# Reciprocal square roots of an attention and MLP kernel, computed as powers on GpSimd in place of a guess and refining steps on VectorE

## The chip, the cores and the metric

The kernel runs on one core of one Trainium2 chip. The metric is the device time of one execution in microseconds (us); the lower, the better. A core has five engines that run side by side, each working through its own instructions in order: TensorE (PE in the profile: matrix products, with the weight loads as PEld), VectorE (DVE), ScalarE (ACT), GpSimd (POOL) and SyncE (SP, which here only starts transfers). They wait for each other by semaphores. Transfers between the chip's main memory (HBM) and the on-chip memory (SBUF), and the transposes in SBUF, run on 16 DMA engines.

## The reference

Attention over 8 batches, 12 heads, 448 tokens and 64 values a head, with q and k normalised, and behind it a gated MLP. What matters here are the two places with a reciprocal square root:

```python
def rmsnorm(x, g):
    rms = np.sqrt(np.mean(x * x, axis=-1, keepdims=True) + 1e-06)
    return x / rms * g
q_n, k_n = (rmsnorm(q, g_q), rmsnorm(k, g_k))
scores = scale * np.matmul(q_n, k_n.transpose(0, 1, 3, 2))
...
mu = np.mean(v, axis=-1, keepdims=True)
var = np.mean((v - mu) ** 2, axis=-1, keepdims=True)
v_n = (v - mu) / np.sqrt(var + 1e-06) * g_ln
```

The first is taken over 64 values for every token and head of q and k, the second over the 512 values of the MLP's v half for every token. Everything is float32.

## The kernel before

The work goes over 48 pairs of heads, six to a batch. A pair has 896 rows of q and 896 of k, as 14 columns of 128 partitions by 64 values. For a pair:

- `squares` (L324, L325): ACT squares the 896 values of each partition, DVE adds them to 14 sums, the tile `ss`.
- `norms` (L335 to L337): the sums of two pairs at a time, 28 columns, become reciprocal roots `ny`. Only the first two pairs are done singly, with 14 columns, so it runs 25 times. On DVE: a scale and add (L335), a guess from the bits of the number in two integer instructions (L107, L108), and seven refining instructions (`newton`, L112 to L118). The tiles are `nx` (the mean square), `ni` (its bits), `nt` (between) and `ny`.
- `split` (L344 to L352): POOL multiplies k by the product of the two gains (L344) and q and k by the roots (L345). ACT takes the float16 high part (L347), POOL the rest (L348), and DVE copies parts into place (L350, L351). A DMA transpose on SP's queue makes `qt` of `hl` (L352). For the first pair all of POOL's part is done on DVE.
- `scores` (L411 to L436): PE multiplies (L411), DVE takes the maximum of a row (L414), ACT the exponential and its sum (L416), DVE the reciprocal of the sums (L420, L422). The high part of the weights is made by ACT (L432) or, for three or four of seven tiles, by POOL (L430), the rest by DVE (L433), and a transpose on SP's queue makes `at` (L436).
- `pv` (L453, L455): PE multiplies the weights with v; ACT and DVE split the result into `xh` and `xl` (L461, L462).

The MLP of a batch (`moe`) runs beside the attention of the next one, a few steps per pair; for the last batch it follows directly. Its `layernorm` takes means and variances (L532, L533, L541 to L545) and then the reciprocal root of four columns, with the same ten DVE instructions: L553, L107, L108, L112 to L118, in the tiles `lx`, `li`, `lt`, `ly`. It runs eight times. L560 applies mean and root, L562 and L563 split the result, and L605 multiplies it. L575 is the product for the other half, u, beside which the layernorm runs.

A third user of the guess, `pow2_scale` (L107, L108, L133 to L135), takes a power of two from it and has no refining steps.

No order of the instructions is written out. The program is traced in the order in which the loops at its end interleave the streams (scores, pv, weights, MLP), each instruction with a place in that order. A planner then simulates the engines with its own costs and puts each engine's instructions into the queue by place and by when they become ready. So a change in one place can move instructions in others.

Of the kernel before, what the change touches and what calls it, by code (L numbers as in the profile page):

```python
# [8 lines left out]
F32 = mybir.dt.float32  # L9
# [13 lines left out]

# places in the order of the work that the MLP and its gelus are moved by
MOFF, MOFF0, GP = 200, 100, 350
# steps of the weights and of the MLP per pair of heads (first, second, middle, last batch)
WR, M0, M1, MR, ML = 3, 8, 7, 11, 11
# pairs of heads at which the first MLP begins and by which the weights are done
I0, WD = 5, 6
# tiles of the scores that share a reciprocal; that are transposed together; whose high part GpSimd  # L30
# makes (in the first batch)
RG = ((0, 2), (2, 4), (4, 7))
TG = (2, 2, 2, 1)
PT, PT0 = (0, 3, 6), (0, 2, 4, 6)
# buffers
NS, NV, NM = 4, 1, 3
# [8 lines left out]
def kernel(  # L45
# [45 lines left out]

# [1 line left out]
    ones = const.tile([P, P], F32, name="ones")  # L93
    G.memset(ones, 1.0)
    ident = const.tile([P, P], BF16, name="ident")
    make_identity(nc, ident)
# [13 lines left out]
    def newton(y, x, t):  # L110
        """y, a guess of x ** -0.5 within 3.5%, made better by a step of third and one of second order."""
        V.tensor_tensor(out=t, in0=x, in1=y, op=ALU.mult)  # L112
        V.tensor_tensor(out=t, in0=t, in1=y, op=ALU.mult)
        V.scalar_tensor_tensor(out=t, in0=t, scalar=-10.0 / 3.0, in1=t, op0=ALU.add, op1=ALU.mult)
        V.scalar_tensor_tensor(out=y, in0=t, scalar=5.0, in1=y, op0=ALU.add, op1=ALU.mult)
        V.scalar_tensor_tensor(out=t, in0=x, scalar=-0.5 * 0.375 ** 3, in1=y, op0=ALU.mult, op1=ALU.mult)
        V.tensor_tensor(out=t, in0=t, in1=y, op=ALU.mult)
        V.scalar_tensor_tensor(out=y, in0=t, scalar=1.5 * 0.375, in1=y, op0=ALU.add, op1=ALU.mult)  # L118

    def pow2_scale(name, part, pool):  # L120
        """part [rows, n] holds sums of squares. Gives the power of two that takes
        every element of the tensor below 2^14 * 1.04, and its inverse."""
        rows, n = part.shape
# [13 lines left out]

# [1 line left out]
    W = {}  # L139

    def decode(dst, raw, tmp):
        """float64 words (low, high) to float32; magnitudes below float32's normal range give 0."""
        hi, lo = raw[:, :, 1], raw[:, :, 0]
# [9 lines left out]
    def weights():  # L153
        nonlocal mlp
        ctx_w = ExitStack()
        # w_in's parts take the place of its float32 values, one K block after the other
        wi = const.tile([P, KT, 2, DF], F16, name="wi")
# [44 lines left out]

        # w_sg with its rows and columns in the order of the tokens on chip, and the
        # last 64 columns twice, so that both halves of the partitions get them
        wsr = [mlp.tile([P, S], F32, name="wsr", tag="ug", bufs=5) for c in range(CK)]
# [48 lines left out]

# [1 line left out]
    # A head's tokens on chip: 128 c + p is token 3 p + c for c < 3 (blocks m0, m1, m2), 384 + p the  # L256
    # tail t. A pair of heads A, B is 7 columns of 128 rows: A's m0, m1, m2, then the tails of A and B
    # in one, then B's m0, m1, m2; so A's keys are in the order (m0, m1, m2, t), B's in (t, m0, m1, m2).
    R = {}
# [31 lines left out]
    def load_v(i):  # L291
        """A head's v in 7 columns: m0, m1, m2, (t, m0a), (m0b, m1a), (m1b, m2a), (m2b, t), with a and b
        the halves of a block: what meets the blocks of A's transposed weights and, from (t, m0a) on, of B's."""
        if i >= NI:
# [16 lines left out]
    def v8(x):  # L311
        """Of a pair's columns A's 0..3 and B's 3..6."""
        return bass.AP(tensor=x.tensor, offset=x.offset, ap=[list(x.ap[0]), [10 * D, 2], [1, 4 * D]])
# [13 lines left out]
    def norms(i, cnt):  # L327
        gi, j = divmod(i, NG)
        n = cnt * SSW
        ss = SS[gi].rearrange("p a b -> p (a b)")[:, j * SSW:j * SSW + n]  # L330
        x, t = (sml.tile([P, NG * SSW], F32, name=f"n{c}", bufs=2)[:, 0:n] for c in "xt")
        si = sml.tile([P, NG * SSW], I32, name="ni", bufs=2)[:, 0:n]
        yt = sml.tile([P, NG * SSW], F32, name="ny", bufs=3)
        y = yf = yt[:, 0:n]
        V.tensor_scalar(out=x, in0=ss, scalar1=1.0 / D, scalar2=1e-6, op0=ALU.mult, op1=ALU.add)  # L335
        rsqrt_guess(yf, si, x)
        newton(yf, x, t)  # L337
        for j in range(cnt):
            R[i + j]["rs"] = y[:, j * SSW:(j + 1) * SSW]
# [17 lines left out]
    def vsquares(i):  # L357
        """The sums of squares of the GV pairs of heads from i on."""
        if i >= NI:
# [29 lines left out]
    def parts_of(t):  # L389
        """Tile t of a pair's 896 rows of scores: (rows of the tile, head)."""  # L390
        if t == CM:
# [73 lines left out]

# [1 line left out]
    def cluster(acts, done):  # L467
        """Gelu activations, one behind the other from when the last one's operand is ready."""
        p = tc.cur_priority
# [15 lines left out]
    def moe(b, early=False):  # L485
# [5 lines left out]
        mv = sml.tile([P, CK, 2], F32, name="mv", bufs=2)  # L491
        # the last 64 tokens have the first half of v in the lower partitions, the second in the upper
        tiles = [(slice(t * P, (t + 1) * P), slice(t * DH, (t + 1) * DH)) for t in range(CM)]
        tiles.append((slice(SM, S), slice(CM * DH, CM * DH + FH)))
        # K block by K block while the batch's last heads are still to come, tile by tile otherwise
        steps = [(t, g) for t in (CM, *range(CM)) for g in range(NP)]
# [39 lines left out]
        def layernorm():  # L536
# [12 lines left out]
            x = sml.tile([P, CK], F32, name="lx", bufs=2)  # L549
            si = sml.tile([P, CK], I32, name="li", bufs=2)  # L550
            y = sml.tile([P, CK], F32, name="ly", bufs=2)
            tt = sml.tile([P, CK], F32, name="lt", bufs=2)
            V.tensor_scalar(out=x, in0=mv[:, :, 1], scalar1=1e-6, scalar2=None, op0=ALU.add)  # L553
            rsqrt_guess(y, si, x)
            newton(y, x, tt)
            vh = mlp.tile([P, CM * DH + FH], F16, name="vh")
# [64 lines left out]
        if b % 2 == 0:  # L621
# [4 lines left out]
            GT[b] = gth, gtl, xt  # L626
        # the last 64 tokens of two batches go together
        for t in range(CM + b % 2):
# [37 lines left out]

# [1 line left out]
    def low(gen, off):  # L668
        """The instructions of a generator, `off` places later in the order."""
        def run():  # L670
# [125 lines left out]
```

## Time and profile before

| what | value |
|---|---|
| median of three runs | 1049.12 us |
| lowest and highest run | 1044.31 and 1051.55 us |
| span of the profiled execution, first to last instruction | 1047.2 us |
| mean granted TensorE clock in it | 0.903 |
| instructions in it | 17092 |
| moved by DMA | 177.74 MB, mean 170 GB/s |
| HBM read and written | 54.58 and 11.01 MB |

The profiled execution's own time is known by its span; what lies around the span is not shown apart from it. The three runs lie 0.7% apart.

How to read the lines that follow: a group's line has the line of the kernel, the engine, the operation, the tile written and the tiles read, the shapes and the count, and then the busy time in us, the mean of one instruction in ns, and the engine's idle time just ahead of such instructions with what ended it. The view by line or tile gives three durations in ns, least, median and greatest, and the first and last start. The view by stage gives the busy time of each engine in a stretch, with the number of instructions in brackets. A timeline row gives start and duration in us, engine, line, operation and tiles. A row of waits gives who waited for whom, the sum in us, how often, and the longest.

### The profile page before, as it was taken

The numbers are of one execution on the slowest core, as the hardware profiler recorded it, in microseconds if no ns is written. First come the engines' busy times: TensorE is split into PE (matmuls) and PEld (weight loads), VectorE is DVE, ScalarE is ACT, GpSimd is POOL, SyncE is SP. The second block draws the span as 40 slices with busy tenths as digits, with TensorE's granted clock in tenths as the row PEclk, the third lists the DMA queues.
The fourth block names the chain that finished last, engine by engine and source line by source line (L and its number), as shares of the span: only waits on it lengthen the run. The fifth ranks groups of instructions, "written<-read, shape, count | busy, mean of one in ns | idle before, by whom it ended". The sixth has DMA issues, their size and how long they took to land. (4 is left out here: it accounts for less than half of the span.)

```text
span 1047.2 us, 17092 instructions
## 1 busy us (share of the span) xinstructions
PE 809.6 (77%) x5652; PEld 447.3 (43%) x5652; DVE 899.9 (86%) x1959; ACT 705.4 (67%) x1418; POOL 504.6 (48%) x435
## 2 busy tenths in 40 slices
PE   0333556757689798888979899887979799799998
PEld 0111222424454346444644357343634365346546
DVE  4999979999789997999979998999889988999430
ACT  2565787676677777677767767587667686877441
POOL 1777745637536463443545372545455443535021
PEclk9666688888899899899999899999989999999999
DMA  5969589685989979996797879994989779838501
GB/s 144 254 174 244 125 179 215 160 185 108 207 180 206 194 156 206 173 217 152 162 213 181 167 149 196 202 211 106 207 190 195 148 166 201 180 89 174 110 1 61
DMA packets 528217, 177.74 MB, mean 170 GB/s; under 512 B 472257, under 2 KB 521985, under 8 KB 528129
## 3 DMA queue, kind: packets, MB, share of 16 engines
q1 hardware_dynamic: 484928, 144.07, 66.6%
q10 hardware_dynamic: 43200, 32.59, 11.3%
q8 instruction: 44, 0.72, 0.3%
q14 instruction: 45, 0.36, 0.1%
HBM read 54.58 MB, written 11.01 MB: 63 GB/s over the span
## 5 line engine op out<-in xcount | busy, mean ns | idle before, releaser
L433 DVE SCALAR_TENSOR_TENSOR ahl<-a,rc,ahl 128x448 f16<-128x448 f32 x336 | 289.6, 886 | 32.1 <-POOL ahl L430 22.0
L416 ACT ACTIVATE a<-s,nm 128x448 f32<-128x448 f32 x336 | 211.0, 630 | 124.7 <-DVE ahl L433 78.0
L411 PE MATMUL s<-qt 128*128 128x448 f16 (+1 forms) x768 | 192.2, 388 | 120.8 <-ACT a L416 63.5
L430 POOL TENSOR_SCALAR ahl<-a,rc 128x448 f16<-128x448 f32 x150 | 117.3, 786 | 230.0 <-DVE rc L422 99.9
L414 DVE TENSOR_REDUCE nm<-s 128x1 f32<-128x448 f32 x336 | 200.2, 610 | 18.5 <-PE s L411 18.0
L432 ACT ACTIVATE ahl<-a,rc 128x448 f16<-128x448 f32 x186 | 118.1, 662 | 61.5 <-DVE rc L422 34.2
L411 PEld LDWEIGHTS <-qt 128*128 128x128 f16 (+1 forms) x768 | 57.2, 105 | 209.2 <-issue 127.8
L345 POOL TENSOR_TENSOR qk<-qk,ny 128x896 f32<-128x896 f32 x47 | 83.2, 1792 | 70.6 <-DVE ny L118 34.4
L348 POOL TENSOR_TENSOR hl<-qk,hl 128x896 f16<-128x896 f32 x47 | 95.7, 2037 | 34.4 <-ACT hl L347 26.3
L453 PE MATMUL pv<-at,vl 128*64 128x384 f16 x384 | 68.2, 368 | 56.7 <-DMA at<-ahl 44.8
L344 POOL TENSOR_TENSOR qk<-qk,gg 128x448 f32<-128x448 f32 x47 | 58.9, 1255 | 77.0 <-ACT sqk L324 76.8
L453 PE MATMUL pv<-at,vh 128*64 128x384 f16 x672 | 91.0, 357 | 0.0
L575 PEld LDWEIGHTS <-wi 128*128 128x128 f16 x576 | 57.4, 102 | 61.8 <-issue 15.9
L455 PE MATMUL pv<-at,vh 128*64 128x64 f16 x672 | 78.7, 202 | 0.0
L611 POOL TENSOR_TENSOR gt<-gt,u 128x448 f32<-128x448 f32 x32 | 39.0, 1221 | 79.0 <-DVE gt L610 59.2
L453 PEld LDWEIGHTS <-vl 128*64 128x64 f16 x384 | 30.7, 118 | 90.0 <-DMA at<-ahl 37.0
L416 ACT ACTIVATION_READ_ACCUMULATOR a<-s,nm 128x1 f32 x336 | 65.9, 196 | 0.0
L325 DVE TENSOR_REDUCE ss<-sqk 128x14 f32<-128x896 f32 x48 | 51.5, 1073 | 15.5 <-ACT sqk L324 15.2
L347 ACT ACTIVATE hl<-qk 128x896 f16<-128x896 f32 x48 | 45.3, 945 | 25.6 <-DMA qk<-in_k_dram 11.4
L324 ACT ACTIVATE sqk<-qk 128x896 f32<-128x896 f32 x48 | 45.3, 944 | 21.7 <-DVE ss L325 11.2
L453 PEld LDWEIGHTS <-vh 128*64 128x64 f16 x672 | 50.2, 120 | 18.6 <-issue 0.8
L420 DVE TENSOR_SCALAR rc<-sums 128x2 f32<-128x2 f32 x144 | 52.1, 364 | 7.1 <-ACT a L416 6.5
(995 smaller groups left out, 2096.0 us busy)
## 6 DMA issues: line engine op xcount, KB each, us to landing
qk<-in_k_dram ACTq DMA_DIRECT2D x48, 192.0 KB, 3.6
vr<-in_v_dram SPq DMA_DIRECT2D x16, 576.0 KB, 4.9
vr<-in_v_dram SPq DMA_DIRECT2D x32, 288.0 KB, 5.9
out_dram<-ot ACTq DMA_DIRECT2D x24, 384.0 KB, 3.8
qk<-in_q_dram ACTq DMA_DIRECT2D x46, 192.0 KB, 3.6
raw<-in_moe_w_in_dram SPq DMA_DIRECT2D x12, 512.0 KB, 4.9
vr<-in_v_dram SPq DMA_DIRECT2D x32, 96.0 KB, 4.9
at<-ahl SPq DMA_TRANSPOSE x192, 3.8
```

The lines of the kernel that those rows point to most:

```text
L344: E.tensor_tensor(out=qk[:, C7:], in0=qk[:, C7:], in1=gg.unsqueeze(1).broadcast_to([P, C7, D]), op=ALU.mult)
L345: E.tensor_tensor(out=qk, in0=qk, in1=r["rs"].unsqueeze(2).broadcast_to([P, SSW, D]), op=ALU.mult)
L348: E.tensor_tensor(out=hl[:, 0:SSW, 1], in0=qk, in1=hl[:, 0:SSW, 0], op=ALU.subtract)
L411: mm(out=ps[p0:p1], lhsT=qt[:, t * P + p0:t * P + p1], rhs=qt[:, k0:k0 + S], start=(n == 0), stop=(n == 1))
L414: V.tensor_reduce(out=nm, in_=ps, axis=AX.X, op=ALU.max, negate=True)
L416: A.activation(out=a, in_=ps, func=AF.Exp, bias=nm, accum_out=sums[:, t - t0:t - t0 + 1])
L430: G.tensor_scalar(out=hl[:, 0], in0=a, scalar1=sc, scalar2=1.0, op0=ALU.mult, op1=ALU.mult)
L432: A.activation(out=hl[:, 0], in_=a, func=AF.Copy, scale=sc)
L433: V.scalar_tensor_tensor(out=hl[:, 1], in0=a, scalar=sc, in1=hl[:, 0], op0=ALU.mult, op1=ALU.subtract)
L453: mm(out=o[:, 0:SM].rearrange("p (c n) -> p c n", c=CM), lhsT=w, rhs=at[:, h * CK:h * CK + CM, blk], start=(n == 0), stop=(n == n_s - 1), ...
L455: mm(out=o[:, SM:S], lhsT=w, rhs=at[:, CM, blk, h * HP:(h + 1) * HP], start=False, stop=(n == n_s - 1), skip_group_check=True)
L575: done = mm(out=ps[:, 0:S], lhsT=ww[:, g, f * P:(f + 1) * P], rhs=xx, start=(n == 0), stop=(n == 17))
```

## The change

Where the roots are made, the ten DVE instructions become two on POOL: a scale and add, and a power with the exponent -0.5. The exponent is read from a constant tile `mhalf` of 128 x 64 that POOL fills at the start. In `norms` the two work on 28 columns (14 for the first two pairs), in the layernorm on four. The layernorm's scale is 1. `nx`, `ni`, `nt`, `li` and `lt` are no longer needed; the norms' mean squares now go to `ny` itself. `rsqrt_guess` stays for `pow2_scale`. `newton` stays in the program and nothing calls it. Comments are dropped.

```diff
     ones = const.tile([P, P], F32, name="ones")
     G.memset(ones, 1.0)
+    mhalf = const.tile([P, 64], F32, name="mhalf")
+    G.memset(mhalf, -0.5)
...
         ss = SS[gi].rearrange("p a b -> p (a b)")[:, j * SSW:j * SSW + n]
-        x, t = (sml.tile([P, NG * SSW], F32, name=f"n{c}", bufs=2)[:, 0:n] for c in "xt")
-        si = sml.tile([P, NG * SSW], I32, name="ni", bufs=2)[:, 0:n]
         yt = sml.tile([P, NG * SSW], F32, name="ny", bufs=3)
-        y = yf = yt[:, 0:n]
-        V.tensor_scalar(out=x, in0=ss, scalar1=1.0 / D, scalar2=1e-6, op0=ALU.mult, op1=ALU.add)
-        rsqrt_guess(yf, si, x)
-        newton(yf, x, t)
+        y = yt[:, 0:n]
+        G.tensor_scalar(out=y, in0=ss, scalar1=1.0 / D, scalar2=1e-6, op0=ALU.mult, op1=ALU.add)
+        G.tensor_tensor(out=y, in0=y, in1=mhalf[:, 0:n], op=ALU.pow)
...
             x = sml.tile([P, CK], F32, name="lx", bufs=2)
-            si = sml.tile([P, CK], I32, name="li", bufs=2)
             y = sml.tile([P, CK], F32, name="ly", bufs=2)
-            tt = sml.tile([P, CK], F32, name="lt", bufs=2)
-            V.tensor_scalar(out=x, in0=mv[:, :, 1], scalar1=1e-6, scalar2=None, op0=ALU.add)
-            rsqrt_guess(y, si, x)
-            newton(y, x, tt)
+            G.tensor_scalar(out=x, in0=mv[:, :, 1], scalar1=1.0, scalar2=1e-6, op0=ALU.mult, op1=ALU.add)
+            G.tensor_tensor(out=y, in0=x, in1=mhalf[:, 0:CK], op=ALU.pow)
```

## The prediction

> **What bounds the kernel now.** I read the page first, for the busy times of the engines, and then the busy time by stage. All times are microseconds unless marked ns.
>
> ```profile
> PE 809.6 (77%) x5652; PEld 447.3 (43%) x5652; DVE 899.9 (86%) x1959; ACT 705.4 (67%) x1418; POOL 504.6 (48%) x435
> ```
>
> The stages, with columns PE, PEld, DVE, ACT, POOL busy (x instructions), granted clock, DMA share, GB/s:
>
> ```profile
> 60.00:300.00 240.00, 144.85 (x926) 74.61 (x926) 221.69 (x462) 164.98 (x334) 143.03 (x113) 0.78 0.80 179
> 300.00:900.00 600.00, 518.58 (x3756) 289.81 (x3753) 547.23 (x1213) 431.66 (x876) 290.17 (x251) 0.94 0.87 183
> 900.00:1047.00 147.00, 133.99 (x942) 79.09 (x940) 86.40 (x195) 82.44 (x160) 44.56 (x45) 1.00 0.41 93
> ```
>
> VectorE (DVE) is busy 92% of the first stretch and 91% of the second; TensorE (PE) 60% and 86%. So DVE alone binds from 60 to 300, DVE with PE close behind from 300 to 900, and in the last 147 us PE (91%) while DVE has slack. What is taken off DVE is worth most early, about half in the middle and nothing at the end.
>
> Third, the ten DVE instructions of each root, by tile and line over the whole span (0 to 60, 60 to 300, 300 to 900, 900 to 1047, and the sum). The three fences are the norms' seven refining steps, their two guess steps and their scale-and-add; the next three the same of the layernorm:
>
> ```profile
> sum 1047.00, DVE 39.07; mean DVE 9.77
> ...
> sum 1047.00, DVE 18.71; mean DVE 4.68
> ...
> sum 1047.00, DVE 8.45; mean DVE 2.11
> ```
>
> ```profile
> sum 1047.00, DVE 15.99; mean DVE 4.00
> ...
> sum 1047.00, DVE 6.20; mean DVE 1.55
> ...
> sum 1047.00, DVE 1.63; mean DVE 0.41
> ```
>
> Together 66.2 for 25 norms and 23.8 for 8 layernorms: 90.0 us of DVE's 899.9 are at stake, in 330 instructions. By stage, the refining steps of the norms and then of the layernorm:
>
> ```profile
> 60.00:300.00 240.00, 8.89 (x35) 0.78 0.80 179
> 300.00:900.00 600.00, 24.16 (x112) 0.94 0.87 183
> ```
>
> ```profile
> 60.00:300.00 240.00, 3.50 (x7) 0.78 0.80 179
> 300.00:900.00 600.00, 10.28 (x35) 0.94 0.87 183
> ```
>
> Of their 55.06, 23% lie in the first stretch, 63% in the second, and the other 14% at the two ends. They last so long partly because they are held up:
>
> ```profile
> L107 DVE TENSOR_SCALAR ni<-nx x25: 156/174/1861, 13.9 to 905.9; 128x28 int32<-128x28 int32 x23, 128x14 int32<-128x14 int32 x2
> ...
> L112 DVE TENSOR_TENSOR nt<-nx,ny x25: 155/174/1829, 14.3 to 908.8; 128x28 f32<-128x28 f32 x23, 128x14 f32<-128x14 f32 x2
> ...
> L112 DVE TENSOR_TENSOR lt<-lx,ly x8: 134/158/565, 206.1 to 1000.7; 128x4 f32<-128x4 f32 x8
> ```
>
> The median is 0.174, the longest 1.8. The timeline shows where such a 1.8 comes from: DVE's L112 starts just behind GpSimd's (POOL's) L348 and ends with it.
>
> ```profile
> 329.59 1.83 DVE L112 TENSOR_TENSOR nt<-nx,ny 128x28 f32<-128x28 f32 x1
> ```
>
> ```profile
> 329.50 1.88 POOL L348 TENSOR_TENSOR hl<-qk,hl 128x896 f16<-128x896 f32 x1
> ```
>
> So a POOL instruction blocks certain DVE instructions until it ends. That is the price list for anything put on POOL.
>
> **The change, part by part.**
>
> *Removed from DVE.* Own time at the medians: 250 x 0.175 + 80 x 0.158 = 56.4. The rest of the 90.0, 33.6, is time held by POOL. It isn't all saved: POOL's other work stays, and the next DVE instruction that needs the same access inherits the wait. Bounds 0 and 33.6; I take half, 16.8. Release: 73.
>
> *Added to POOL: the price of a step.* No row shows a power. The nearest two-input rows are these:
>
> ```profile
> L615 POOL TENSOR_TENSOR gtl<-gt,gh x32: 317/699/792, 250.7 to 1024.6; 128x64 fp32r<-128x64 f32 x32
> ...
> L611 POOL TENSOR_TENSOR gt<-gt,u x32: 1130/1144/1528, 243.2 to 1021.0; 128x448 f32<-128x448 f32 x32
> ```
>
> From the minima: (1130 - 317) / 384 = 2.12 ns a column on 181 ns fixed. One plain pass over 28 columns is 0.24; that is my price of the scale-and-add (4 columns: 0.19) and the lower bound of the power. A power must be made of many arithmetic steps (a logarithm, a product, an exponential); DVE's own root takes nine. My estimate is twenty steps at 2.12 ns x 28: 1.19 + 0.18 = 1.37 (4 columns: 0.35). The upper end of this case is sixty steps, 3.74. I take twenty because the nearest row that computes the same thing, DVE's nine, is nearer to it than to sixty. Added to POOL: 25 x 1.61 + 8 x 0.54 = 44.6; POOL goes from 505 to about 549 of 1047 and is not a bound by its own busy time.
>
> *What that blocks on DVE.* How much DVE loses to POOL today shows in the groups' means (the number after the busy time) against their medians (the middle one of three):
>
> ```profile
> L433 DVE SCALAR_TENSOR_TENSOR ahl<-a,rc,ahl 128x448 f16<-128x448 f32 x336 | 289.6, 886 | 32.1 <-POOL ahl L430 22.0 <-ACT ahl L432 10.1
> ...
> L420 DVE TENSOR_SCALAR rc<-sums 128x2 f32<-128x2 f32 x144 | 52.1, 364 | 7.1 <-ACT a L416 6.5
> ```
>
> ```profile
> L433 DVE SCALAR_TENSOR_TENSOR ahl<-a,rc,ahl x336: 658/676/2397, 40.9 to 977.9; 128x448 f16<-128x448 f32 x168
> ...
> L420 DVE TENSOR_SCALAR rc<-sums x144: 128/159/1698, 34.3 to 975.5; 128x2 f32<-128x2 f32 x96, 128x3 f32<-128x3 f32 x48
> ```
>
> Held: L433 71, L420 30 and the 34 above: 135 us by 505 us of POOL, 0.27 a us. At that rate 44.6 costs DVE 12. A longer stretch of POOL work blocks a larger part, all but the first 0.6 or so that one unblocked DVE instruction fills: 25 x (1.61 - 0.6) = 25. Bounds 12 and 44.6; I take 20, since the power stands next to two L345 that block already. Net release: 73 - 20 = 53.
>
> *What it is worth.* I weigh the first stretch 0.9, the second 0.55 and the ends 0.2: 0.23 x 0.9 + 0.63 x 0.55 + 0.14 x 0.2 = 0.58 of the net, 31 us. The 0.55 is a choice: 63% of 53 is 33, and if all of it came off, PE's 519 would fill 91% of 567, as tight as DVE is now.
>
> *The wait that moves.* The power now stands in POOL's queue and waits there for DVE's L325. Behind it wait the same pair's L345, then L430, for which DVE's L433 waits, for which ACT's L416 waits. Before, POOL stood waiting for the end of DVE's chain:
>
> ```profile
> POOL qk L344 <- ACT sqk L324: 76.8, 24, 19.1
> ...
> PE s L411 <- DMA qt<-hl: 51.8, 9, 27.5
> ...
> POOL qk L345 <- DVE ny L118: 34.4, 11, 8.4
> ...
> DVE ahl L433 <- POOL ahl L430: 22.0, 28, 3.6
> ```
>
> The new wait is short, since the L324 squares that L344 waits for also start L325, and the result is there earlier. I cost it at nothing; without that cover each us that POOL's queue loses ahead of an L430 adds to the last row. What falls due next is L347 on ACT and the transpose qt on SP's queue; no DMA is moved or added.
>
> *Start and tail.* The first pair's root leaves DVE about 1.8 us sooner, but ACT, which follows with L347, is issuing loads until 18.6:
>
> ```profile
> 15.75 1.09 DVE L345 TENSOR_TENSOR qk<-qk,ny 128x896 f32<-128x896 f32 x1
> ...
> 17.96 0.63 ACTq L269 DMA_DIRECT2D qk<-in_q_dram  x1
> 18.69 0.95 ACT L347 ACTIVATE hl<-qk 128x896 f16<-128x896 f32 x1 [11.44 <-DMA qk<-in_k_dram]
> ```
>
> Nothing gained; uncovered it would be 1.8. The last layernorm ends on DVE at 1002.0, while the chain that ended last runs on PE over it, up to the first matmul of L605 at 1007.5:
>
> ```profile
> 1001.85 0.16 DVE L118 SCALAR_TENSOR_TENSOR ly<-lt,ly 128x4 f32<-128x4 f32 x1
> ```
>
> ```profile
> 1003.36 0.95 PE mu__12133 L575 x5
> ...
> 1007.52 0.38 PE ms__12159 L605 x2
> ```
>
> Also nothing; a slow power has 5 us there. The added memset of 128x64 lies under the first loads: nothing.
>
> *Sum.* 1047.2 - 31 = 1016; the profiled span is 1.9 below the median of 1049.1, so 1018 on the scale of the runs.
>
> *Rules that bear on it.* The Trainium skill (Perfetto Trace Analysis, Optimizing Scalar/DVE Operations) warns that VectorE and GpSimd share an SBUF read port, "so offloading operations between those two might not help". The L112 row beside L348 agrees; taken at its word it is the second rival below. The Trainium skill (GPSIMD Engine Reference, Performance pitfalls for Q7 kernels) puts an fp32 dependent chain at 4 cycles an element and step; an estimate from that page, twenty steps at 1.2 GHz over 28 columns, is 1.9 instead of 1.2, and the time would be 1018 + 0.58 x 25 x 0.7 = 1028. No trace here shows it.
>
> **The rivals.**
>
> 1. *Slow power* (the other side). If GpSimd makes the power element by element, it blocks POOL and with it DVE for all but 0.6 of its length. It decides from 25 x (d + 0.24 - 0.6) = 73, so d = 3.3 us per norm. At a hundred steps, 6.1, it costs 144 - 73 = 71 us of DVE; lengthening the bound engine counts more fully, 0.8: +57, 1106. For it: no row bounds the power from above. Against: even L348, the longest POOL kind, does 896 columns in 1.9.
>
> 2. *The block takes it back.* All 33.6 held go on to other instructions and all 44.6 of new POOL time blocks: 56.4 - 44.6 = 12, worth 7: 1042. For it: DVE's queue is full, so a block always meets someone. Against: the reduction L414, 336 times on DVE, shows no long case, so not all of DVE's work meets the block:
>
> ```profile
> L414 DVE TENSOR_REDUCE nm<-s x336: 584/610/626, 28.8 to 973.5; 128x1 f32<-128x448 f32 x168
> ```
>
> 3. *Cheap power and a shorter chain.* At one step the block is 5, net 68, worth 39; and a root that is ready earlier takes about 10 off PE's waits for qt: 1000. For it: one chain runs on the crowded DVE from 354.7 to 361.1, and POOL stands 7.5 us for it. Against: two qt buffers limit how far ahead the norms may run.
>
> ```profile
> 354.73 0.17 DVE L335 TENSOR_SCALAR nx<-ss 128x28 f32<-128x28 f32 x1
> ...
> 360.92 0.19 DVE L118 SCALAR_TENSOR_TENSOR ny<-nt,ny 128x28 f32<-128x28 f32 x1
> ```
>
> ```profile
> 361.24 1.69 POOL L345 TENSOR_TENSOR qk<-qk,ny 128x896 f32<-128x896 f32 x1 [7.52 <-DVE ny L118]
> ```
>
> 4. *It doesn't do what it says*, the power coming as two passes of that price: 25 x (2.98 - 0.6) = 60 of block, net 13, worth 8: 1041. For it: nothing in these rows. Against: one source line is one row throughout this profile.
>
> **How the numbers follow.** Forecast 0.43 (own range 1000 to 1038), slow power 0.23, block 0.17, cheap power 0.15, the last 0.02. Low end: net 68 with all held time returned, 85, at 0.65 is 55: 994, and 4 for a changed order of issue, 990. High end: half of the slow case must lie inside, 1095. A measurement here tells about 1%, 10 us, from none. Faster by more: 0.40 of the forecast, 0.15 of cheap, 0.03 of block: 0.58. Slower: 0.22 of the slow power. Within: the other 0.20.
>
> **What would show it.** DVE loses 330 instructions and about 50 to 70 us of busy time; POOL gains 66 instructions; the power's row is 1 to 2 us; L433's mean stays near 0.89; POOL's wait for L118 is gone with no like wait on L325. Wrong: a power row over 3.3, an L433 mean over 1.0, DVE less busy while PE and ACT wait longer for L433.

## The result, and the profile after

The kernel after takes 1060.7 us (median of four runs, 1056.7 to 1065.6) against 1048.2 for the kernel before, also four runs. The ratio is 1.0127, with a 95% interval of 1.0094 to 1.0161: 1.3% slower, where 31 us less were forecast. The profiled execution of after is that of 1065.6 us, the longest of the four, with a span of 1063.8, against 1047.2 of before. Its mean granted TensorE clock is 0.900 against 0.903; over the four runs of after it is 0.880 to 0.900, mean 0.891, and over the 70 runs of before that stood beside the experiments 0.892 to 0.920, mean 0.904. Among those 70 a run with 0.01 less clock was 1.2 us longer in the mean, so an estimate from them puts about 2 us of the difference on the clock; no run parts that from the rest.

The busy times of the page of after:

```profile
PE 821.7 (77%) x5652; PEld 448.2 (42%) x5652; DVE 864.3 (81%) x1629; ACT 704.2 (66%) x1420; POOL 641.2 (60%) x502
```

DVE has lost its 330 instructions, but its busy time fell by only 35.6 us, where they lasted 90.0. POOL has gained 67 instructions (66 and the memset) and 136.6 us, where 44.6 were forecast. The lines that made most of these 136.6, by line and form, with busy time, mean ns of one, and the idle time ahead of them:

```profile
L336 POOL TENSOR_TENSOR ny<-ny,mhalf 128x28 f32<-128x28 f32 x23 | 112.7, 4901 | 1.2
L551 POOL TENSOR_TENSOR ly<-lx,mhalf 128x4 f32<-128x4 f32 x8 | 9.2, 1150 | 0.4
L335 POOL TENSOR_SCALAR ny<-ss 128x28 f32<-128x28 f32 x23 | 8.2, 356 | 31.1 <-DVE ss L327 20.5 <-DVE rc L419 5.9 <-DVE rc L421 2.0
L336 POOL TENSOR_TENSOR ny<-ny,mhalf 128x14 f32<-128x14 f32 x2 | 5.2, 2598 | 0.2
```

One power over 28 columns takes 4.9 us, over 14 columns 2.6, over four 1.15. From size to size that is 145 to 165 ns for each further column; the plain pass beside it (L335) takes 0.36 for all 28.

Part of the 90.0 was never DVE's alone. Rows of DVE overlap: one starts while the row ahead of it still lasts. Two of the root's rows of before, each with the row behind it:

```profile
355.87 0.14 DVE L114 SCALAR_TENSOR_TENSOR lt<-lt 128x4 f32<-128x4 f32 x1
355.94 0.28 DVE L351 COPY hl<-hl 128x448 f16<-128x448 f16 x1
...
356.67 0.16 DVE L107 TENSOR_SCALAR ni<-nx 128x28 int32<-128x28 int32 x1
356.75 0.28 DVE L350 COPY hl<-hl 128x448 f16<-128x448 f16 x1
```

Without the root's 330 rows, those of before cover 843.9 us and not 899.9. So only 56.0 us of the busy time were the root's alone, and after has 864.3.

Did the power hold DVE up, as POOL's L344 and L347 (before: L345 and L348) do? The timeline of after, a power first, with the instruction behind it, and two of DVE's instructions under it:

```profile
437.62 4.80 POOL L336 TENSOR_TENSOR ny<-ny,mhalf 128x28 f32<-128x28 f32 x1
442.42 0.63 POOL L429 TENSOR_SCALAR ahl<-a,rc 128x448 f16<-128x448 f32 x1
```

```profile
438.12 0.68 DVE L432 SCALAR_TENSOR_TENSOR ahl<-a,rc,ahl 128x448 f16<-128x448 f32 x1
438.72 0.75 DVE L385 SCALAR_TENSOR_TENSOR vl<-vr,v_s,vh 128x512 f16<-128x512 f32 x1
```

And 5 us later the same two lines of DVE, under POOL's L344:

```profile
443.02 3.71 POOL L344 TENSOR_TENSOR qk<-qk,ny 128x896 f32<-128x896 f32 x2
```

```profile
443.09 2.10 DVE L432 SCALAR_TENSOR_TENSOR ahl<-a,rc,ahl 128x448 f16<-128x448 f32 x1 [0.61 <-POOL ahl L429]
445.11 2.17 DVE L385 SCALAR_TENSOR_TENSOR vl<-vr,v_s,vh 128x512 f16<-128x512 f32 x1
```

Under the power they last 0.68 and 0.75, under L344 three times that. It is so everywhere in this profile: 27 L432 start inside a power and at least 0.9 us ahead of its end, and all last at most 0.69; 34 start so inside an L344 or L347, and all last 1.4 or more. The only thing that DVE suffers from this power is in the bracket of the last fence: 0.61 of waiting for L429, which stood behind it in POOL's queue. What became longer on DVE:

```profile
L432 DVE SCALAR_TENSOR_TENSOR ahl<-a,rc,ahl 128x448 f16<-128x448 f32 x336 | 304.2, 932 | 31.7 <-POOL ahl L429 21.1 <-ACT ahl L431 10.0
...
L385 DVE SCALAR_TENSOR_TENSOR vl<-vr,v_s,vh 128x512 f16<-128x512 f32 x48 | 53.4, 1112 | 1.3 <-ACT vh L383 1.3
```

L432 (before L433) lasts 932 ns where it lasted 886: 14.6 us more in all, and L385 6.1 more (47.3 before). These two means alone tell little, since the four orders of before that follow below have 884 to 923 ns for L433 and the three orders of after 898 to 932 for L432. What all of DVE's other instructions last above their own medians tells more: 158 us in before and 180 in after (158 to 167 and 178 to 180 over the orders). So 22 of the 33.6 us for which POOL held the root have come back on other instructions.

The waits of after, with the sum in us, how often, and the longest:

```profile
PE s L410 <- DMA qt<-hl: 88.2, 12, 26.0
...
ACT a L415 <- DVE ahl L432: 84.4, 72, 4.9
...
PE s L410 <- ACT a L415: 46.7, 35, 3.8
...
POOL lx L550 <- DVE mv L544: 36.0, 5, 24.9
ACT ahl L431 <- DVE rc L421: 35.0, 27, 4.7
...
POOL ny L335 <- DVE ss L327: 27.8, 9, 6.1
```

POOL's 34.4 us of waiting for the end of DVE's root (L118) are gone. In their place it stands 27.8 us for the sums and 36.0 for the layernorm's variances, most of the latter once, 24.9 us. PE waits 88.2 us for the transposed q and k instead of 51.8.

Where along the span was the time lost? As marks serve the starts of `xh`, of which each pair of heads has one, behind its `pv`: the 13th (twelve pairs are done) and the 47th (46 are done). The stages between them, before, with columns as in the prediction:

```profile
0.00:337.45 337.45, 193.78 (x1240) 97.46 (x1241) 302.37 (x636) 220.76 (x441) 190.36 (x156) 0.80 0.81 182
337.45:977.11 639.66, 552.91 (x4009) 311.16 (x4009) 583.14 (x1285) 461.81 (x945) 304.20 (x268) 0.95 0.83 177
977.11:1047.20 70.09, 62.91 (x406) 38.64 (x404) 14.36 (x40) 22.85 (x36) 10.07 (x12) 0.99 0.17 44
```

and after:

```profile
0.00:352.85 352.85, 196.32 (x1242) 96.61 (x1243) 289.24 (x533) 221.81 (x443) 235.42 (x177) 0.81 0.77 174
352.85:990.56 637.71, 560.00 (x4004) 311.83 (x4002) 561.55 (x1064) 458.00 (x943) 393.87 (x311) 0.94 0.84 177
990.56:1063.80 73.24, 65.39 (x410) 39.77 (x409) 13.54 (x32) 24.34 (x40) 11.89 (x15) 0.97 0.17 44
```

The first twelve pairs take 15.4 us longer, the next 34 take 2.0 less, the tail 3.2 more. So the loss is early, where DVE's relief was weighed highest, and in the long middle relief and cost nearly cancel.

### The profile page after: what moved, and what is told of

Its sections match the earlier page's. It is cut to its first block, busy times and chain, and to the rows that moved or that the text cites. A ratio compares the mean times of both kernels' runs of the same rounds, so it can differ in the third digit from the quotient of the medians.

```text
span 1063.8 us, 16789 instructions
## 1 busy us (share of the span) xinstructions
PE 821.7 (77%) x5652; PEld 448.2 (42%) x5652; DVE 864.3 (81%) x1629; ACT 704.2 (66%) x1420; POOL 641.2 (60%) x502
## 5 line engine op out<-in xcount | busy, mean ns | idle before, releaser
L432 DVE SCALAR_TENSOR_TENSOR ahl<-a,rc,ahl 128x448 f16<-128x448 f32 x336 | 304.2, 932 | 31.7 <-POOL ahl L429 21.1
L410 PE MATMUL s<-qt 128*128 128x448 f16 (+1 forms) x768 | 195.2, 396 | 136.1 <-DMA qt<-hl 88.2
L415 ACT ACTIVATE a<-s,nm 128x448 f32<-128x448 f32 x336 | 210.7, 630 | 128.6 <-DVE ahl L432 84.4
L429 POOL TENSOR_SCALAR ahl<-a,rc 128x448 f16<-128x448 f32 x150 | 111.2, 745 | 200.5 <-DVE rc L421 80.7
L410 PEld LDWEIGHTS <-qt 128*128 128x128 f16 (+1 forms) x768 | 57.7, 107 | 227.6 <-issue 115.3
L336 POOL TENSOR_TENSOR ny<-ny,mhalf 128x28 f32<-128x28 f32 (+1 forms) x25 | 117.9, 4717 | 1.3
L452 PE MATMUL pv<-at,vl 128*64 128x384 f16 x384 | 65.2, 354 | 42.4 <-DMA at<-ahl 31.1
L347 POOL TENSOR_TENSOR hl<-qk,hl 128x896 f16<-128x896 f32 x47 | 95.6, 2034 | 2.2 <-ACT hl L346 1.6
L452 PE MATMUL pv<-at,vh 128*64 128x384 f16 x672 | 88.8, 350 | 0.0
L344 POOL TENSOR_TENSOR qk<-qk,ny 128x896 f32<-128x896 f32 x47 | 87.8, 1887 | 0.2
L454 PE MATMUL pv<-at,vh 128*64 128x64 f16 x672 | 77.3, 201 | 0.0
L415 ACT ACTIVATION_READ_ACCUMULATOR a<-s,nm 128x1 f32 x336 | 66.5, 198 | 0.0
L327 DVE TENSOR_REDUCE ss<-sqk 128x14 f32<-128x896 f32 x48 | 51.5, 1073 | 14.6 <-ACT sqk L326 14.5
L383 ACT ACTIVATE vh<-vr,v_s 128x896 f16<-128x896 f32 x48 | 49.8, 1039 | 9.1 <-issue 2.6
```

The lines of the kernel that those rows point to most:

```text
L336: G.tensor_tensor(out=y, in0=y, in1=mhalf[:, 0:n], op=ALU.pow)
L344: E.tensor_tensor(out=qk, in0=qk, in1=r["rs"].unsqueeze(2).broadcast_to([P, SSW, D]), op=ALU.mult)
L347: E.tensor_tensor(out=hl[:, 0:SSW, 1], in0=qk, in1=hl[:, 0:SSW, 0], op=ALU.subtract)
L410: mm(out=ps[p0:p1], lhsT=qt[:, t * P + p0:t * P + p1], rhs=qt[:, k0:k0 + S], start=(n == 0), stop=(n == 1))
L415: A.activation(out=a, in_=ps, func=AF.Exp, bias=nm, accum_out=sums[:, t - t0:t - t0 + 1])
L429: G.tensor_scalar(out=hl[:, 0], in0=a, scalar1=sc, scalar2=1.0, op0=ALU.mult, op1=ALU.mult)
```

## The experiments

Three causes could make up the result, and the runs were chosen to part them. The first is the time that the power takes on POOL. The second is that DVE's relief is worth little. The third is the order: any change lets the planner put all engines' instructions in another order, and that order may be better or worse by chance or by what the planner takes an operation to cost. A fourth, the granted clock, had no run of its own.

### The power made cheap, the order kept

In three kernels the norms' power is a copy of the same columns, so the norms' roots are left out; the layernorms keep their powers. The planner is told that this copy costs what a power costs, so that it makes the same order: in the traces DVE, ACT and SP have line by line the order of the kernel with the power, and on POOL the copies stand where the powers stood. The first has the order of after, the others those of two more kernels "after" (r7, r8 below).

```diff
-        G.tensor_tensor(out=y, in0=y, in1=mhalf[:, 0:n], op=ALU.pow)
+        G.tensor_copy(out=y, in_=y)
```

> The changed kernel with the power of the norms replaced by a plain copy of the 28 columns on GpSimd, every engine's instructions in exactly the order of the changed kernel (the planner is told that the copy costs what the power costs); q and k are scaled by their mean squares, not by the roots. Queue theory (the power holds up what stands behind it in GpSimd's queue, and the transposes of q and k): about 115 us of GpSimd time go, the time falls below the kernel before, to 1020 to 1035, PE's wait for qt falls from 88 us to about 50, and the mean of the weights' subtraction on DVE (L432, 932 ns) stays within 30 ns. Block theory (the power holds DVE's two-input instructions while it runs): the time falls likewise, but that mean falls to 890 or less. Order theory (the planner's other order costs the time, not the power itself): 1055 to 1065.

> The kernel after in the nudged order of the second after (price of an addition on GpSimd 96 ns), with the norms' power replaced by a copy of the same columns and every engine's order kept, so the norms' roots are not taken. Theory A (the power's time on GpSimd costs some 13 us in any order): 1068.7 less 13, 1053 to 1058, 1.003 to 1.008 of before. Theory B (the 13 us belong to one order, where the copy happened to fit well): within 4 us of 1068.7, so 1065 to 1073. Theory C (GpSimd's time is what the whole loss comes from, whatever the order): down to before's time, 1046 to 1051.

> The same replacement in the order of the third after (price of a multiplication 96 ns, 1064.3 us with its powers): the norms' power is a copy, the roots are not taken, every engine keeps its order. Theory A (the power costs some 13 us in any order): 1049 to 1054. Theory B (only in one order): 1060 to 1068. Theory C (all of the loss is GpSimd's time): 1046 to 1051, which A's range can't be told from here, only in the run beside it.

| order | with powers, ratio to before | with copies, ratio to before | difference |
|---|---|---|---|
| of after | 1.0127 [1.0094, 1.0161] | r1: 1.0002 [0.998, 1.0025], 1047.9 us | 1.25%, 13.1 us |
| of r7 | 1.0187 [1.0114, 1.026] | r9: 1.0052 [1.0031, 1.0073], 1055.1 us | 1.35%, 14.1 us |
| of r8 | 1.0145 [1.0076, 1.0214] | r10: 1.0011 [0.9981, 1.0041], 1052.8 us | 1.34%, 14.0 us |

The copy, against 4.81 us of the power, and DVE's L432 beside it, in r1:

```profile
L336 POOL COPY ny<-ny x25: 195/207/669, 8.1 to 904.5; 128x28 f32<-128x28 f32 x23, 128x14 f32<-128x14 f32 x2
...
L432 DVE SCALAR_TENSOR_TENSOR ahl<-a,rc,ahl 128x448 f16<-128x448 f32 x336 | 307.6, 942 | 28.7 <-POOL ahl L429 18.3 <-ACT ahl L431 9.9
```

The power's time on POOL costs 13 to 14 us in three different orders. That is shown by edits that change nothing else but the numbers in q and k. By the intervals each difference is sure to 0.4% (r1) or 0.8% (r9 and r10, as r7 and r8 have two runs each); with copies the clock is 0.90, so here too about 1 us may be the clock's. None of r1's three expectations was met as a whole: the time fell, but not to 1035, and the wait for `qt` hardly moved. r9 and r10 came out as their Theory A says, and r10 lies in no range but that one. The stages of r1, with their sum:

```profile
0.00:348.18 348.18, 195.61 (x1240) 97.44 (x1240) 289.20 (x527) 221.87 (x443) 198.42 (x179) 0.80 0.78 176
348.18:971.83 623.65, 555.10 (x4004) 310.30 (x4003) 548.53 (x1071) 456.96 (x942) 322.56 (x308) 0.95 0.86 182
971.83:1045.10 73.27, 65.46 (x410) 39.89 (x409) 13.54 (x32) 24.34 (x40) 11.89 (x15) 0.97 0.16 43
sum 1045.10, PE 816.17 PEld 447.62 DVE 851.27 ACT 703.17 POOL 532.87; mean PE 272.06 PEld 149.21 DVE 283.76 ACT 234.39 POOL 177.62
```

POOL works 108 us less than in after, so one us of the power costs 0.12 to 0.13 us of time. In the middle stage r1 is 16.0 us faster than before, with 34.6 us less of DVE; early it is 10.7 slower. Who waited for the power? In the waits of r1, against those of after above:

```profile
PE s L410 <- DMA qt<-hl: 82.0, 11, 25.0
...
POOL ahl L429 <- ACT a L415: 57.7, 18, 7.3
...
POOL hl L347 <- ACT hl L346: 29.1, 13, 5.9
...
ACT ahl L431 <- DVE rc L421: 22.1, 22, 2.8
...
DVE ahl L432 <- POOL ahl L429: 18.3, 25, 1.2
```

The greater part of the power's 108 us lay in idle time of POOL, which is 512.3 us with the copy and 422.6 with the power: its wait for ACT ahead of L347 is 29.1 and 1.6, its wait for the exponentials of L415 57.7 and 37.6. What got through to PE is spread: 6.2 more on `qt` here (5.5 and 3.6 in the other two pairs), and 2.8 (3.9, 3.3) on DVE's wait for L429. No single wait holds the 13 us. L432 lasts 942 ns with copies, 932 with powers: the longer L432 isn't the power's doing.

### The order alone

Five kernels have the same instructions as before or after, and only one price in the planner's list is moved by 3 ns: an addition on GpSimd, 93 in the list, is 96 in r5 and r7 and 90 in r6; a multiplication is 96 in r8 and r12. The order of the engines' instructions changes with it.

```diff
+... _D['Add'] = (96, 2); ...
```

> The kernel before, instruction for instruction, but the planner is told that a GpSimd add or subtract costs 3 ns more (96 for 93 fixed), so that it chooses another order on every engine. If the order by itself matters (the times so far of 1061, 1081 and 1087 for kernels with the same 25 powers say so): more than 1% from 1048, and more likely slower, since the order of the kernel before has been chosen among others. If it doesn't: 1043 to 1053.

> As r5_before_j1, with 3 ns less (90 for 93). Order matters: 1058 to 1085, and not the same as r5_before_j1. Order doesn't: 1043 to 1053.

> The kernel before, the same instructions, in the order that comes out with a multiplication on GpSimd priced at 96 ns. Theory 1 (order alone moves this kernel by 1 to 2% and the order of before is one of its better ones): 1053 to 1070. Theory 2 (an order costs nothing, and what two nudged orders showed was an exception): 1046 to 1051.

> The changed kernel, instruction for instruction, with the planner's add or subtract at 96 for 93. Order matters: more than 1% from 1061, 1050 to 1090. Order doesn't: 1056 to 1066.

> As r7_after_j1, with the planner's GpSimd multiplication at 96 for 93 instead. Order matters: more than 1% from 1061 and from r7_after_j1. Order doesn't: 1056 to 1066.

The kernel before took 1.007 [1.0025, 1.0115], 1.019 [1.0119, 1.0261] and 1.004 [1.0017, 1.0063] of itself (1055.6, 1069.1 and 1052.8 us), and the kernel after 1.0187 and 1.0145 of before (1068.7, 1064.3 us; intervals in the table above). So the order is worth up to 1.9% here (r6, two runs), more than the whole change, and the order of before is the best of its four. Of the five only r6 moved by more than the 1% that the expectations named: r5 and r12 lie 0.7 and 0.4% above before, and r7 and r8 can't be told from after. The mean of the four befores is 1.0075, that of the three afters 1.0153: over orders the change costs 0.8%, not 1.3%, and that is sure to about half a per cent.

### The other parts

In r2 both powers are multiplications and the planner prices them as such; in r3 the kernel before gets 33 powers that nothing uses; in r4 the norms have their powers and the layernorm is back on DVE.

```diff
-        G.tensor_tensor(out=y, in0=y, in1=mhalf[:, 0:n], op=ALU.pow)
+        G.tensor_tensor(out=y, in0=y, in1=mhalf[:, 0:n], op=ALU.mult)
...
-            G.tensor_tensor(out=y, in0=x, in1=mhalf[:, 0:CK], op=ALU.pow)
+            G.tensor_tensor(out=y, in0=x, in1=mhalf[:, 0:CK], op=ALU.mult)
```

> The changed kernel with both powers replaced by multiplications with the same constant tile, planned by the cost of a multiplication, so in an order of its own; no roots are taken. Queue theory: as the copy, 1020 to 1035, within 1% of it. Order theory: more than 1% from the copy, either way. If what DVE gives up is worth nothing (PE and ACT bind): 1043 to 1053, the same as before.

```diff
+        dz = sml.tile([P, NG * SSW], F32, name="dz", bufs=2)[:, 0:n]
+        G.tensor_tensor(out=dz, in0=x, in1=mhalf[:, 0:n], op=ALU.pow)
...
```

> The kernel before, roots on VectorE as they were, plus the 33 powers on GpSimd into tiles that nothing reads: GpSimd's time of the change without the relief of DVE and without a place in the chain of q and k. Queue theory: slower than before by 15 to 30 us, 1063 to 1080, the mean of L433 within 30 ns of 886. Block theory: that mean over 950 and DVE's busy time up by 60 us or more. Order theory, or a harm that lies in the chain of q and k alone: 1043 to 1055.

```diff
-            G.tensor_scalar(out=x, in0=mv[:, :, 1], scalar1=1.0, scalar2=1e-6, op0=ALU.mult, op1=ALU.add)
-            G.tensor_tensor(out=y, in0=x, in1=mhalf[:, 0:CK], op=ALU.pow)
...
+            V.tensor_scalar(out=x, in0=mv[:, :, 1], scalar1=1e-6, scalar2=None, op0=ALU.add)
+            rsqrt_guess(y, si, x)
+            newton(y, x, tt)
```

> Only the norms as powers; the layernorm's roots stay on VectorE. All theories: 1055 to 1065 if the norms carry the loss. If the layernorm's powers, for which 36 us of GpSimd's idle time are waits, carry it: 1040 to 1050.

Measured: r2 1052.2 us, 1.0054 [1.0028, 1.008]; r3 1081.1, 1.0322 [1.0274, 1.037]; r4 1087.0, 1.0367 [1.0321, 1.0412]. By r3 the powers cost 33 us, by the copies 13 to 14. r3 has an order of its own, so it can't give the price; it lies 3.2% above before, beyond what the nudges moved, with DVE as busy as ever (906 us). In it nothing reads what the powers make, and DVE isn't held more: the weights' subtraction lasts 906 ns, where the block theory had asked for over 950 and 60 us more of DVE. r2 met only the expectation that the relief is worth nothing (1043 to 1053). r4 is 2.4% slower than after, outside both of its ranges, though only the layernorms' DVE instructions came back; it loses in the first twelve pairs (356.6 us) and most in the middle (656.0). Its order is its own too, but it lies outside what the nudged orders showed, and its cause stays open.

### The relief by itself

Four kernels are before without the seven refining steps: 231 of the 330 instructions leave DVE and nothing goes to POOL. The roots are then right to 3.5%. One has the planner's own order, three the nudges of r5, r6 and r12. Two more are r2 with two of the nudges.

```diff
-        newton(yf, x, t)
...
-            newton(y, x, tt)
```

> The kernel before with the two refining steps left out behind every guess (7 instructions x 33 on VectorE, 231 of the 330 that the change takes away), nothing put on GpSimd in their place; roots are right to 3.5% only. Its order is the planner's own. Theory 1 (VectorE's time is not what sets the pace, and its relief is worth less than what an order moves): 1040 to 1062, VectorE's busy time some 25 to 45 us less. Theory 2 (as predicted: relief of VectorE pays 0.58 of what its groups give up, and GpSimd ate it in the change): 231/330 of 73 us x 0.58 is 30 us, so 1014 to 1027.

> The kernel before without the refining steps (231 instructions of VectorE's 330, roots right to 3.5%), in the order that an addition priced at 96 ns gives; the kernel before in an order nudged in the same way took 1.007 of before. Theory 1 (the relief itself is worth some 10 us, in any order): 0.997 of before, 1044 to 1050. Theory 2 (nothing; the 0.990 of the first such kernel was a good order): 1053 to 1062. Theory 3 (as predicted, 30 us): 1020 to 1032.

> The same without the refining steps, with an addition priced at 90 ns; before took 1.019 of itself under that nudge. The order comes out near that of the first kernel without steps, so Theory 1 (the relief is worth some 10 us): 1036 to 1046, Theory 2 (nothing, and the 0.990 was order): 0.990 again, as the order is nearly the same, so this run tells little between them; Theory 3 (30 us): below 1032.

> The same without the refining steps, with a multiplication priced at 96 ns; before took 1.004 of itself under that nudge. Theory 1 (relief worth some 10 us in any order): 0.994 of before, 1040 to 1047. Theory 2 (nothing): 1050 to 1058. Theory 3 (30 us): 1018 to 1030.

> Both powers replaced by a multiplication of the same shape (no roots are taken), the order the planner's own, with an addition on GpSimd priced at 96 ns. The start of the 13th xh marks the end of the early stretch: 332 to 346 us in the four kernels before, 345 to 350 in the three with copies whose order was made for the power's price, 336 in the first kernel with multiplications. Theory 1 (the early loss of the copies is the order that the planner made for a dear power): 332 to 341. Theory 2 (it is the root standing in GpSimd's queue): 344 to 352. Time from there to the 47th xh: 624 to 634 if the relief is worth some 15 us there, 640 to 647 if nothing. Whole time 1040 to 1056.

> The same with a multiplication on GpSimd priced at 96 ns. Theory 1: the 13th xh at 332 to 341; Theory 2: at 344 to 352. From there to the 47th xh 624 to 634 if the relief is worth some 15 us there, 640 to 647 if nothing. Whole time 1040 to 1056.

Without refining steps: 0.9903 [0.9869, 0.9936], 0.9915 [0.9881, 0.995], 0.9897 [0.9851, 0.9942] and 1.0091 [1.0057, 1.0126] of before, 1040.0, 1043.6, 1040.1 and 1059.9 us. With multiplications: 0.9926 [0.9898, 0.9954] and 1.0067 [1.0042, 1.0093], 1040.0 and 1055.2 us. r14 lies in the range expected for a relief of 10 us and r13 just below its own (1044); r11 lies at the foot of its range for a small relief (1040); r15 lies above even the range for no relief; r17 stands for 10 us, r18 for little; none for 30. So the value can only be a mean: 0.9952 without steps and 1.0016 for the three with multiplications, against 1.0075 for before over its orders, 13 and 6 us. With three or four orders each, up to 2% apart, these means are sure to about half a per cent. The relief is worth something between little and 20 us; none of the ten kernels with a relieved DVE and nothing dear on POOL came near the 31 forecast, and the best is 10.1 us below before.

The stages part it further. Time to the 13th `xh`, from there to the 47th, and the rest, read from the same rows of each profile; the lists are the orders, in the order in which the kernels stand above:

| kernels | first twelve pairs | next 34 | tail | mean of each |
|---|---|---|---|---|
| before, r5, r6, r12 | 337.5, 332.3, 346.3, 332.0 | 639.7, 644.2, 647.0, 641.5 | 70.1, 77.3, 74.8, 71.4 | 337.0, 643.1, 73.4 |
| after, r7, r8 | 352.9, 354.9, 352.5 | 637.7, 641.0, 636.0 | 73.2, 72.1, 73.4 | 353.4, 638.2, 72.9 |
| copies: r1, r9, r10 | 348.2, 349.7, 345.3 | 623.7, 629.0, 626.0 | 73.3, 72.1, 73.6 | 347.7, 626.2, 73.0 |
| multiplications: r2, r17, r18 | 336.0, 337.2, 335.5 | 632.7, 632.5, 644.0 | 79.0, 72.8, 73.7 | 336.2, 636.4, 75.2 |
| no steps: r11, r13, r14, r15 | 332.9, 339.4, 337.4, 337.2 | 625.4, 629.3, 628.7, 651.5 | 75.6, 73.3, 71.4, 73.4 | 336.7, 633.7, 73.4 |

Read down the means. In the middle the relief gives 7 to 17 us and the power takes 12 back. In the first twelve pairs the relief gives nothing that shows: 336.2 and 336.7 against 337.0, with 13 us less of DVE there in r2 (289.60 against 302.37); the four befores lie 14 us apart there, so a relief of a few us can't be ruled out. There the copies lose 10.7 us although their copy takes 0.2 us, as a multiplication does; what they have and the multiplications don't, beside the layernorms' 9 us of powers, is the order that the planner makes for a power that it prices as dear. That decides between the two causes put against each other in r17 and r18: 337.2 and 335.5 are in the order's range, 344 to 352 would have been that of the mere place in POOL's queue. In the middle r17 fell into the range for a relief of 15 us (632.5) and r18 into that for none (644.0). The power itself adds 5.7 early. These are single executions, and after less copies comes to 17.6 us in them where the medians say 13 to 14, so the parts are to be read as shares. The early 11 us show in PE's waits for `qt`. Ahead of the 13th `xh` these come to 35 to 47 us in the four befores, 41 to 49 without steps, 52 to 53 with multiplications, 73 to 76 with copies and 77 to 81 with powers, most of it in the first 150 us. So of the 36.4 us by which this wait grew from before to after, only 6 are the power's. Which instruction's place in that order makes `qt` late isn't found; r6 has 346.3 early without any power, so other orders do it too.

### A version between the two

r16 leaves the guess on DVE and puts the refining steps on POOL, as ten plain instructions for each root, so that the roots are refined as before.

```diff
+    def newton_g(y, x, t):
+        G.tensor_tensor(out=t, in0=x, in1=y, op=ALU.mult)
+        G.tensor_tensor(out=t, in0=t, in1=y, op=ALU.mult)
...
-        newton(yf, x, t)
+        newton_g(y, x, t)
...
-            newton(y, x, tt)
+            newton_g(y, x, tt)
```

> A version that might beat both: the guess stays on VectorE (three instructions), the refining steps go to GpSimd as ten plain instructions for each root, 330 in all at some 0.24 us by the row of L348, so about 80 us on GpSimd in place of 127 us of the two powers; the roots are right. Theory A (GpSimd's time costs in proportion, 13 us for 118): 10 us off for VectorE, 9 us on for GpSimd, 1045 to 1053 and no gain. Theory B (a chain of ten on an engine that waits in order holds its users longer than one long instruction): over 1055.

Measured: 1064.3 us, 1.0133 [1.01, 1.0166]. Its dearest and its cheapest step by the groups:

```profile
L125 POOL TENSOR_TENSOR nt<-nw,nt 128x28 f32<-128x28 f32 (+1 forms) x25 | 11.2, 449 | 1.7
...
L131 POOL TENSOR_TENSOR ny<-nt,ny 128x28 f32<-128x28 f32 (+1 forms) x25 | 7.6, 306 | 1.8
```

At 0.31 to 0.45 us a step over 28 columns and not 0.24, POOL's busy time is 606.9, between before's 504.6 and after's 641.2, and the time is that of after. It is over 1055, as the expectation had it for a chain that holds its users longer; but its order is its own, so the chain's part isn't shown. No kernel that makes the full roots was found below before.

## Why the prediction was wrong, by its own steps

**What bounds.** "DVE alone binds from 60 to 300" failed. The kernels with 231 or 330 instructions less reach the 13th `xh` no sooner than before over its orders. A busy share of 92% didn't show that an engine sets the pace; the relief's 0.9 there, 0.23 x 0.9 x 53 = 11 us, was worth under 1 us in the means. What sets the pace there isn't found.

**Removed from DVE.** 330 instructions, as said. The release of 73 failed, and the step is the 90.0 that it starts from. That counts whole rows, as the 56.4 of own time does, and of the busy time only 56.0 us were the root's alone, held time included. DVE's busy time fell by 35.6, and by 48.6 in r1, where nothing dear stood in the norms. The half of the held 33.6 that was let go to other instructions was near the mark: 22 us in after, and 9 in r1 (158 to 168).

**The price of a power.** This is the term of the sum that was mis-sized most, and it made the kernel slower: with copies in its place r1, r9 and r10 lie 0.0 to 0.5% above before. 1.37 us was taken and 3.74 was the upper end of the case; 4.9 was measured, 0.35 against 1.15 at four columns, and POOL got 136.6 us and not 44.6. At the 2.12 ns a column of a plain pass that is about 79 steps, not 20: DVE's nine instructions were no measure of what GpSimd does for the same root. The Trainium skill (GPSIMD Engine Reference, Performance pitfalls for Q7 kernels) puts a step of a dependent chain at 4 cycles; an estimate from that page, 49 steps at 1.2 GHz for the 165 ns a column, would fit, but no run shows the steps. The prediction's own sign of failure, "a power row over 3.3", was met.

**What that blocks on DVE.** 20 us were charged, and in the slow case all but 0.6 of each power. None was found: 27 of 27 L432 under a power are unheld. The mechanism of the first rival is refuted though its side of the sum came out. By its formula 4.9 us gives 25 x (4.9 + 0.24 - 0.6) = 114 on DVE, less 73, times 0.8: +32 us, 1081, and 1061 was measured. What the power costs is its time in POOL's queue: what stands behind it, or waits for its root, comes later. No run parts these two; r3, where nothing reads what they make, is slower as well.

**The wait that moves.** It was costed at nothing, with the remark that each us that POOL's queue loses ahead of an L430 adds to DVE's wait. L335 now waits 27.8 us and L550 36.0, while POOL's waits for L118 (34.4) went. But the kernels with copies and multiplications have waits of the same kind (23.8 on L335 in r1, 17.1 in r17) and are no slower than the mean of before over its orders. So no cost of that wait shows, though it may have eaten part of the relief. The queue behind a slow power was left out: 13 to 14 us.

**What it is worth.** The middle term held best: 0.63 x 0.55 x 53 = 18 us was forecast, and copies, missing steps and multiplications give 17, 9 and 7 there in the mean. That the first meets the 18 is partly luck: for each us by which DVE's busy time in that stage lies under the mean of the four befores, they gain 0.43, 0.39 and 0.25 us, under the 0.55. The power took 12 of it.

**The order.** Put at 4 us in the low end of the range and nowhere else. It moves before by up to 19 us, and the order made for a dear power costs 11 in the first twelve pairs. With the measured numbers over orders: 17 gained in the middle, 12 and 6 paid for the power, 11 for the order early; with the tails that is 11 lost in the profiled spans, and 8 by the medians (0.8%). The other 5 us of the measured 12.6 are orders: that of before lies 0.75% under the mean of its four, that of after 0.26% under the mean of its three.

**Of the rivals.** The slow power gave the sign and the wrong mechanism; the block that takes it back let all 33.6 held us and all of POOL's new time come back on DVE, and 22 of the first and nothing of the power did; the cheap power with a shorter chain isn't borne out, since PE's waits for `qt` are 82.0 in r1 and 59.0 in r2, not less than 51.8; the fourth is refuted, as L336 is one row.

## What to carry to other kernels

Before an operation is moved to GpSimd, time that operation there at its size: a power over 28 columns took fourteen times the plain pass beside it. Removing work from the busiest engine pays only where that engine sets the pace, and a share of 90% doesn't show that; try it with a kernel that merely leaves the work out. Where a planner makes the order, run both kernels in several orders before a per cent is believed, and price a single operation by replacing it with a cheap one that the planner is told is as dear.

## What the runs showed of the hardware that wasn't expected

A power on GpSimd took 4.9 us over 28 columns of 128 partitions and 145 to 165 ns for each further column. Although it reads two tiles in SBUF like L344, it held up none of the 27 L432 that started well inside its 4.8 us, while L344 and L347 held all 34 that met them so to 1.4 to 2.3. The Trainium skill (SBUF — State Buffer, Who interferes with whom) has GpSimd and such a DVE instruction exclude one another until the first has finished; L344's rows agree, the power's (0.68 inside 4.80) do not; why isn't shown. And rows of DVE overlap: 330 rows that last 90.0 us together covered only 56.0 us that no other row covered.
